# A down-projection by seven block products in place of eight, with token tiles in pairs

## The chip, the cores and the metric

The kernel runs on one core of one Trainium2 chip. The metric is the device time of one launch in microseconds (us). The kernel before takes 586.73 us (median of three runs, 585.8 to 587.77).

## What is computed

Two blocks follow each other, all in fp32: a gated linear recurrence (attention), and a Fourier mixing block with a two-layer projection behind it. Shapes: batch 4, 8 heads, 768 tokens, 48 channels a head, so 384 channels for the second block, and 1536 hidden units.

```python
f = 1 / (1 + exp(-f_logit))                        # attention, per batch and head
for t in range(S):
    state = f[t][:, None] * state + outer(k[t], v[t])
    y[t] = q[t] @ state
x = heads side by side                             # (4, 768, 384)
mixed = real(fft(fft(x, axis=1), axis=2))
u = x + mixed
un = (u - mean(u)) / sqrt(var(u) + 1e-6)           # over the channels
out = u + maximum(un @ w_ch1, 0) @ w_ch2           # 384 -> 1536 -> 384
```

The two weight matrices arrive as 64-bit floats and are turned into fp32 on the chip.

## The kernel before

**Units and batches.** Attention is done in 16 units, each a pair of heads of one batch; four units make a batch. Unit u's steps are, in order: exponentials on ScalarE (ACT), a scan on VectorE (DVE), more exponentials, the products `q` and `W` on DVE (L302, L303), 48 score matmuls `sc` (L314), a masked copy on DVE (L321), transposes `st` (L459), `ds` matmuls (L470), a state scan on DVE (L478), two sets of `y` matmuls (L490, L497), transposes `yt` (L517), and a fold of the tokens (DVE and GpSimd, POOL). The inputs of a unit are loaded by SP's queue: `f`, `k`, `q` two transfers each (L152), `v` one (L148).

**Fourier mixing and projection.** For each batch, `fnet` does four `z` steps (matmuls with a sequence table, L602), three `mix` steps (L618) whose results DVE adds to `x`, and the moments of each row. `turn` normalises a tile of 128 tokens into `un` (L653) and transposes it (`pt`, L656) into `unT`. A batch has six token tiles. Before, they go in two halves of three: for each half 12 steps `up`, each three matmuls with 384 moving columns (three tiles side by side, L690) and a ReLU on ACT into `h1` (L693), then for each of its three tiles 12 matmuls `po` (L700), a sum over the 12 blocks of hidden units with 384 output columns. DVE adds the sum to `x` (L704), and `store` writes the tile: tiles 1, 2, 3 and 5 by an indirect transfer from POOL's queue (L570), tiles 0 and 4 by SP (L576). Tile 4 comes last in its batch. Its rows go to two places, row 0 to one and rows 1 to 127 to the other.

**Buffers.** All PSUM tiles of `fnet` (`z`, `mix`, `pt`, `pp` of the up-projection, `po`) have the tag "f" and take turns in two buffers. `h1` has 13 buffers of 384 columns, the raw weights (`raw`) three.

**Weights and tables.** The weights come in 24 blocks of 384 KB. A word `C` converts one block (L209 and L210 on DVE, L219 and L220 on ACT, L222 on POOL); a word `c` looks at its smallest entry (L270 on DVE) and fetches a later block; `R` fetches the first three. The first 12 blocks are `w1`, the others `w2`. `tables` (word `T`) loads the tables of cosines: `seq_tab`'s first part with 128 rows (L157), its second with 127 rows (L158) and one row (L159), then the `wave` rows, 97, 63 and 33 of them (L170 to L172). `sort_tables` (word `S`) prepares them on POOL.

**What sets the order.** The text `ORDER` is a schedule written out by hand, and each engine executes its own instructions in the order in which they are issued there. A number is the next step of that unit, `F`b the next step of batch b's `fnet`, `H`b the next step of its `turns`, `L` a load (unit, then what), `G` clears a gap, `I` and `Z` set constants, `M` judges at the end whether the inputs ask for a second, slower way (the branch under `again`, which is not taken here).

Of the kernel before, what the change touches and what calls it, by code (L numbers as in the profile page):

```python
# [12 lines left out]
C = 128  # L13
# [30 lines left out]
)  # L44


@with_exitstack
def kernel(
# [36 lines left out]
    ph1 = ctx.enter_context(tc.tile_pool(name="ph1", bufs=13))  # L85
# [68 lines left out]
    def tables():  # L154


        nc.sync.dma_start(out=tab[:, 0, 0], in_=seq_tab[:, 0, 0])  # L157
        nc.sync.dma_start(out=tab[1:128, 0, 1], in_=seq_tab[1:128, 0, 1])  # L158
# [12 lines left out]
        nc.sync.dma_start(out=wave[1][0:63], in_=dim_tab[65:128, 1])  # L171
        nc.sync.dma_start(out=wave[1][63:QD], in_=dim_tab[0:QD - 63, 2])  # L172
        return wave
# [69 lines left out]
    def words(i):  # L243
        _, src, cols = blocks_of[i]
        raw = pr.tile([128, 384, 2], U32, tag="raw", name=f"raw{i}")
# [19 lines left out]
    def sizes():  # L265
# [7 lines left out]
        looked[0] += 1  # L273

# [53 lines left out]
    def attention_by_blocks(u, x_all):  # L328
# [8 lines left out]
        AD = ph1.tile([128, 2, NCH, 32], F32, tag="h1", name=f"ad{u}")  # L337
# [229 lines left out]
    def store(b, c, rows):  # L567
# [7 lines left out]
        for i, j, o in {0: [(0, C, 0)], 4: [(0, 1, 3 * QS), (1, C, HS + 1)]}[c]:  # L575
            nc.sync.dma_start(out=out[b, o:o + j - i], in_=rows[i:j])  # L576

    behind = {}

    def fnet(b, x, again=False):  # L580
# [66 lines left out]
        turned = [None, None]  # L647

        def turn(c):
            if c % 3 == 0:  # L650
                turned[c // 3] = p2.tile([128, 3, 3 * 128], F32, tag="unT", name=f"unT{b}_{c // 3}")
# [3 lines left out]
            for kt in range(3):  # L655
                nc.tensor.transpose(pt[:, kt * 128:(kt + 1) * 128], un[:, kt * 128:(kt + 1) * 128], ident)  # L656
            nc.scalar.copy(turned[c // 3][:, :, c % 3 * 128:(c % 3 + 1) * 128],  # L657
                           pt[:, :DM].rearrange("p (k t) -> p k t", k=3))

        def turns():  # L660
            for c in range(NCH):
                if c == 3:
                    for i in range(3, NCH):
                        moments(i)
                    deviation(slice(3, NCH))
                    yield
                turn(c)
                yield

        behind[b] = turns()  # L670
# [10 lines left out]
        for half in range(2):  # L681
            if again:
                for _ in behind[b]:
                    pass
            unT = turned[half]
            h1 = []
            for m in range(NF):
                pp = ps_f.tile([128, 512], F32, tag="f", name=f"up{b}_{half}_{m}")
                for kt in range(3):
                    nc.tensor.matmul(pp[:, :3 * 128], lhsT=w1[:, kt, m * 128:(m + 1) * 128], rhs=unT[:, kt],  # L690
                                     start=(kt == 0), stop=(kt == 2))
                h = ph1.tile([128, 3 * 128], F32, tag="h1", name=f"h1_{b}_{half}_{m}")
                nc.scalar.activation(h, pp[:, :3 * 128], AF.Relu)  # L693
                h1.append(h)
                yield
            for i in ((0, 1, 2), (0, 2, 1))[half]:
                c = 3 * half + i
                po = ps_f.tile([128, 512], F32, tag="f", name=f"po{b}_{c}")
                for m in range(NF):
                    nc.tensor.matmul(po[:, :DM], lhsT=h1[m][:, i * 128:(i + 1) * 128], rhs=w2[:, m],  # L700
                                     start=(m == 0), stop=(m == NF - 1))
                    if m in (3, 7):
                        yield
                nc.vector.tensor_tensor(x[:, c], po[:, :DM], x[:, c], ALU.add)  # L704
                store(b, c, x[:, c])
                yield

    x_of, units, fronts = {}, {}, {}
# [24 lines left out]
    with tc.manual_schedule():  # L733
        for word in ORDER.split():
# [5 lines left out]
            elif kind == "F":  # L740
                if n not in fronts:
                    fronts[n] = fnet(n, x_of.pop(n))
                next(fronts[n], None)
            elif kind == "H":
# [25 lines left out]
    with tc.If(again > 0):  # L770
        if wide:
            for i, (dst, _, _) in enumerate(blocks_of):
                single_or_zero(dst, words(i))
        nc.sync.dma_start(out=causal.rearrange("p (i n) -> p i n", n=32), in_=sel)
        for u in range(4):
            load(u, *("fkqv" if u < 3 else "qv"))
        for b in range(B):
# [4 lines left out]
            for _ in fnet(b, x, again=True):  # L782
                pass
# [69 lines left out]
```

## Time and profile before

| What | us |
|---|---|
| median of three runs | 586.73 |
| the profiled execution | 586.55 |
| its span, first to last instruction | 584.8 |
| PE (TensorE matmul) busy | 536.4 |
| DVE busy | 241.0 |
| ACT busy | 193.5 |
| POOL busy | 90.6 |

The span is what the profile sees, and the profiled execution's own time is 1.75 us longer. Busy times of the engines overlap, so they don't add up to the span. The trace leaves two records for each fp32 matmul: 288 matmuls of the up-projection stand as 576 rows of L690, and likewise for L700. A record's mean duration holds the pipeline's depth, so records that follow each other closely start at smaller distances than their mean durations. PEld is the loading of weights into PE, SPq the issuing of transfers by SP.

### The profile page before, as it was taken

To read this page: it belongs to the slowest core of one execution; us is meant where nothing else is said; L and a number is where in the kernel's file an instruction comes from. 1 tells how busy PE (TensorE), PEld (TensorE's weight loads), DVE (VectorE), ACT (ScalarE), POOL (GpSimd) and SP (SyncE) were. 2 spreads that over 40 slices of the span, in tenths; PEclk is the share of its full clock that TensorE was granted. 3 is DMA by queue.
4 is the path that set the end of the run, shared out by engine and by line. 5 is a ranking of instruction groups with operands and counts; after the bars stand their busy time and mean duration, and the time that the engine had idled before them with its cause. 6 is when DMAs were issued, how large, how long until landed. Compare 5 with 4: busy or idle time off the path is not lost.

```text
span 584.8 us, 8503 instructions
## 1 busy us (share of the span) xinstructions
PE 536.4 (92%) x3450; PEld 350.4 (60%) x3450; DVE 241.0 (41%) x431; ACT 193.5 (33%) x441; POOL 90.6 (15%) x147
## 2 busy tenths in 40 slices
PE   0778399999999999999999999999999999999991
PEld 0656276666566666766567666666565555555550
DVE  8997599975736334532526213111322020010000
ACT  5786057875425232631143301421123003102100
POOL 5335312434400000101100010220100000010010
PEclk9998599999999999999999999999999999999996
DMA  8974166651511021004300000000000000000000
GB/s 230 230 193 139 48 186 164 191 163 55 149 41 40 1 68 47 10 1 114 89 2 1 1 27 8 7 0 16 27 2 0 15 20 7 15 13 13 2 29 17
DMA packets 14785, 34.83 MB, mean 60 GB/s; under 512 B 2575, under 2 KB 4176, under 8 KB 14736
## 3 DMA queue, kind: packets, MB, share of 16 engines
q1 hardware_dynamic: 13632, 30.65, 19.5%
q0 software_dynamic: 1104, 3.54, 1.7%
q8 instruction: 29, 0.48, 0.4%
q14 instruction: 20, 0.16, 0.1%
HBM read 29.46 MB, written 4.72 MB: 58 GB/s over the span
## 4 chain that ended last, share of the span: by engine, by line
PE 84%; DMA 3%; DVE 3%; ACT 3%; SPq 2%; issue 2%; POOL 1%; ACTq 0%; DVEq 0%; POOLq 0%
PE up L690 33%; PE po L700 32%; PE z L602 4%; PE sc L314 3%; PE y L490 3%; PE y L497 2%; PE mix L618 2%; DMA q<-in_qkf_dram 2%; PE pt L656 1%; PE ds L470 1%; PE yt L517 1%; SPq L171 1%; DMA v<-in_v_dram 1%; PE st L459 1%; DMA g<-in_qkf_dram 1%
## 5 line engine op out<-in xcount | busy, mean ns | idle before, releaser
L690 PE MATMUL up<-unT,w 128*128 128x384 f32 x576 | 195.1, 490 | 1.3 <-ACT h L693 0.6
L700 PE MATMUL po<-w,h 128*128 128x384 f32 x576 | 189.8, 487 | 0.0
L700 PEld LDWEIGHTS po<-w,h 128*128 128x128 f32 x576 | 108.2, 190 | 73.4 <-issue 0.3
L690 PEld LDWEIGHTS up<-unT,w 128*128 128x128 f32 x576 | 106.8, 190 | 71.7 <-issue 1.2
L693 ACT ACTIVATE h<-up 128x384 f32<-128x384 f32 x96 | 46.9, 489 | 197.7 <-PE up L690 197.5
L704 DVE TENSOR_TENSOR x<-po,x 128x384 f32<-128x384 f32 x24 | 13.4, 557 | 156.5 <-PE po L700 156.5
L314 PE MATMUL sc<-q,W 48*64 48x128 f32 x768 | 29.1, 302 | 27.7 <-DVE W L303 23.1
L570 POOL DMA_INDIRECT out_dram<-x,place x16 | 16.5, 1033 | 229.2 <-DVE x L704 216.4
L314 PEld LDWEIGHTS sc<-q,W 48*64 48x64 f32 x768 | 24.3, 149 | 33.0 <-issue 15.7
L321 DVE COPY_PREDICATED at<-causal,sc 128x768 f32<-128x768 uint32 x32 | 31.4, 1034 | 16.9 <-PE sc L314 16.9
L222 POOL TENSOR_TENSOR w<-w,raw 128x384 uint32<-128x384 uint32 x24 | 27.5, 1148 | 52.2 <-ACT raw L220 41.0
L290 DVE TENSOR_TENSOR_SCAN W<-g,bound 112x768 f32<-112x768 f32 x16 | 28.2, 1761 | 8.6 <-PE st L459 7.6
L490 PE MATMUL y<-at,v 128*64 128x128 f32 (+1 forms) x384 | 27.0, 294 | 0.0
L490 PEld LDWEIGHTS y<-at,v 128*64 128x64 f32 (+1 forms) x384 | 23.2, 140 | 4.2 <-issue 3.4
L302 DVE TENSOR_TENSOR q<-q,g 112x768 f32<-112x768 f32 x16 | 16.7, 1041 | 20.3 <-ACT g L295 12.8
L292 POOL COPY deep<-W 112x1 f32<-112x1 f32 x16 | 5.4, 338 | 123.4 <-DVE W L290 123.2
L478 DVE TENSOR_TENSOR_SCAN stt<-ds,te 112x288 f32<-112x288 f32 x16 | 11.9, 751 | 28.6 <-PE ds L470 28.6
L497 PE MATMUL y<-q,stt 48*48 48x128 f32 x320 | 21.3, 276 | 0.0
L497 PEld LDWEIGHTS y<-q,stt 48*48 48x48 f32 x320 | 17.9, 159 | 5.0 <-issue 3.3
L657 ACT COPY unT<-pt 128x384 f32<-128x384 f32 x24 | 11.4, 481 | 25.2 <-PE pt L656 25.2
L618 PE MATMUL mix<-cd,zz 96*128 96x192 f32 (+5 forms) x128 | 18.4, 331 | 0.7 <-ACT h L693 0.5
L210 DVE SCALAR_TENSOR_TENSOR w<-raw,w 128x384 uint32<-128x384 uint32 x24 | 17.8, 742 | 0.8
(116 smaller groups left out, 486.6 us busy)
## 6 DMA issues: line engine op xcount, KB each, us to landing
raw<-in_w_ch_dram SPq DMA_DIRECT2D x24, 384.0 KB
v<-in_v_dram SPq DMA_DIRECT2D x16, 288.0 KB
g<-in_qkf_dram SPq DMA_DIRECT2D x32, 144.0 KB
q<-in_qkf_dram SPq DMA_DIRECT2D x32, 144.0 KB
k<-in_qkf_dram SPq DMA_DIRECT2D x32, 144.0 KB
out_dram<-x SPq DMA_DIRECT2D x4, 192.0 KB
out_dram<-x SPq DMA_DIRECT2D x4, 190.5 KB
out_dram<-x,place POOLq DMA_INDIRECT x16, 2.6
```

The source lines that it names most:

```text
L210: nc.vector.scalar_tensor_tensor(bits, hi, 0xC0000000, bits, ALU.bitwise_and, ALU.bitwise_or)
L222: nc.gpsimd.tensor_tensor(bits, bits, lo, ALU.add)
L290: nc.vector.tensor_tensor_scan(W, g, bound[:R], 0.0, ALU.add, ALU.min)
L314: nc.tensor.matmul(ps[64 * s:64 * s + 64, r, i * C:(i + 1) * C], lhsT=W[ROWS[r], o + 64 * s:o + 64 * s + 64], rhs=Q[ROWS[r], o:o + C], sta ...
L321: nc.vector.copy_predicated(AT[:, :, half], causal.bitcast(U32).unsqueeze(1).unsqueeze(1).to_broadcast([128, 2, NCH // 2, C]), ps[:, :, :N ...
L490: nc.tensor.matmul(y[FILL[r], c * C:(c + 1) * C], lhsT=vt[:, c, r * D:r * D + (64 if r == 0 else D)], rhs=AT[:, r, c], start=(c % 4 == 0), ...
L497: nc.tensor.matmul(y[ROWS[r], c * C:(c + 1) * C], lhsT=st[ROWS[r], :, c - 1], rhs=Q[ROWS[r], c * C:(c + 1) * C], start=False, stop=True, s ...
L602: nc.tensor.matmul(z[:, cols], lhsT=src[:, j, lo:hi], rhs=tab[:, t, T % 2, cols], start=(i == 0), stop=(i == len(parts) - 1), skip_group_c ...
L618: nc.tensor.matmul(mix[rows, o], lhsT=zz[:rows_of[T], T, j:j + rows.stop - rows.start], rhs=cd[:rows_of[T], T, :NQ - odd], start=(i == 0), ...
L690: nc.tensor.matmul(pp[:, :3 * 128], lhsT=w1[:, kt, m * 128:(m + 1) * 128], rhs=unT[:, kt], start=(kt == 0), stop=(kt == 2))
L693: nc.scalar.activation(h, pp[:, :3 * 128], AF.Relu)
L700: nc.tensor.matmul(po[:, :DM], lhsT=h1[m][:, i * 128:(i + 1) * 128], rhs=w2[:, m], start=(m == 0), stop=(m == NF - 1))
```

## The change

**Seven products.** The token tiles go in pairs, (0, 3), (2, 5) and (1, 4), and the hidden units in two halves of six blocks. For a pair, the ReLU outputs are four blocks h11, h21 (first half of the hidden units, first and second tile) and h12, h22 (second half), and `w2` is four blocks w11, w12 (first half of the hidden units, left and right 192 output columns) and w21, w22. The plain way takes eight block products. The new function `combine` (word `W`, once) makes, on DVE,

T1 = w12 - w11, T2 = w22 - T1, T3 = w22 - w12, T4 = w21 - T2,

and `projected` makes for each pair, on DVE as well,

S1 = h21 + h22, S2 = S1 - h11, S3 = h11 - h21, S4 = h12 - S2.

With seven products, in the order in which they are issued, P1 = h11 w11, P2 = h12 w21, P4 = h22 T4, P5 = S1 T1, P6 = S2 T2, P3 = S4 w22, P7 = S3 T3, the results are

first tile, left: P1 + P2; right: P1 + P6 + P5 + P3; second tile, left: P1 + P6 + P7 + P4; right: P1 + P6 + P7 + P5.

Each product is six matmuls of 192 moving columns. The sums are kept in two PSUM tiles, `fx` (P1, to which P6 and then P7 are added, and P2) and `fz` (P4, and P5 with P3). DVE adds each part to `x` as it becomes ready, and the last addition (`both`) adds the sum of P1, P6 and P7 to both halves of the second tile.

**What goes with it.** `up` steps have 256 moving columns (two tiles) and `h1` two buffers of six blocks. The first pair of the first batch still takes the plain way, 24 matmuls of 384 columns, since its turn comes before all of `w2` is there. `fnet` ends after the `mix` steps, and the rest of a batch has the word `P`: 20 steps a pair, 12 `up` and then eight. `turns` and the moments are regrouped for the pairs. The order is new from its first word on: `R` comes first, and `W` after the second pair's last `up` step. Tile 4 still comes last in its batch.

**Row sixteen.** The 127 rows of tile 4's second store, and the 127 rows of one load of `seq_tab`, are cut into rows 1 to 15 and 16 to 127.

```diff
 ORDER = (
-    "Gq0 L0v Gq2 Gk2 Gq3 I L0f 0 Gk1 Gk0 L1f L0q Gq1 0 L1k i 1 L0k R Z 0 L1q 1 0 1 C C L3fk c 0 0 0 L2f "
...
+    "R Gk0 I Gq0 i L0f Gq1 L1f Gq2 Gk2 Z L2q Gq3 L0q C L2f C Gk1 L0k C c c 0 0 1 0 1 0 C L1k L1q L2v 0 "
+    "L0v c 0 1 0 L2k 2 C L3fk 0 1 L1v c 0 1 0 3 C 0 2 1 1 L3v 3 2 1 1 3 2 0 L3q 1 3 2 2 L4fk 4 c 3 3 "
+    "L5fk 2 1 0 3 C C 2 2 T 2 1 2 L4qv 3 4 c c 1 3 5 L6fk 3 c 2 4 L5qv 3 3 5 4 2 5 4 4 4 3 5 6 S 4 C 4 4 "
...
+    "P2 P2 P2 P2 F3 P2 P2 F3 F3 P2 F3 P2 P2 P2 F3 P2 P2 P2 P2 P2 P2 P2 P2 P2 H3 P2 P2 P2 H3 P2 P2 P2 H3 "
+    "P2 P2 P2 P2 P2 F3 F3 P2 P2 P2 P2 H3 P2 P2 P2 P2 P3 P3 P3 H3 H3 P3 P3 P3 P3 P3 P3 P3 P3 P3 P3 P3 P3 "
+    "P3 P3 P3 P3 P3 P3 P3 P3 P3 P3 P3 H3 P3 P3 P3 P3 P3 P3 H3 P3 P3 P3 P3 P3 P3 P3 P3 P3 P3 P3 P3 P3 P3 "
+    "P3 P3 M P3 P3 P3 P3 P3 P3 P3 P3 P3 P3 P3 P3"
 )
+
+PAIRS = ((0, 3), (2, 5), (1, 4))
...
-    ph1 = ctx.enter_context(tc.tile_pool(name="ph1", bufs=13))
+    ph1 = ctx.enter_context(tc.tile_pool(name="ph1", bufs=2))
...
-        nc.sync.dma_start(out=tab[1:128, 0, 1], in_=seq_tab[1:128, 0, 1])
+        nc.sync.dma_start(out=tab[1:16, 0, 1], in_=seq_tab[1:16, 0, 1])
+        nc.sync.dma_start(out=tab[16:128, 0, 1], in_=seq_tab[16:128, 0, 1])
...
+    def combine():
+        H = NF // 2
+        w11, w12, w21, w22 = [w2[:, i * H:(i + 1) * H, j * HD:(j + 1) * HD] for i in range(2) for j in range(2)]
+        t2, t3, t4 = [pr.tile([128, H, HD], F32, tag="raw", name=f"block{i}") for i in range(3)]
+        tt = nc.vector.tensor_tensor
+        tt(t3, w22, w12, ALU.subtract)
+        tt(w12, w12, w11, ALU.subtract)
+        tt(t2, w22, w12, ALU.subtract)
+        tt(t4, w21, t2, ALU.subtract)
+        blocks[1], blocks[2], blocks[4] = w11, w21, t4
+        blocks[5], blocks[6], blocks[3], blocks[7] = w12, t2, w22, t3
...
-        for i, j, o in {0: [(0, C, 0)], 4: [(0, 1, 3 * QS), (1, C, HS + 1)]}[c]:
+        for i, j, o in {0: [(0, C, 0)], 4: [(0, 1, 3 * QS), (1, 16, HS + 1), (16, C, HS + 16)]}[c]:
...
+    def projected(b, x, again=False):
+        H = NF // 2
+        tt = nc.vector.tensor_tensor
+        for j, (c, d) in enumerate(PAIRS):
...
+            unT = turned_of[b][j].rearrange("p k t n -> p k (t n)")
+            hs = []
             for m in range(NF):
-                pp = ps_f.tile([128, 512], F32, tag="f", name=f"up{b}_{half}_{m}")
+                if m % H == 0:
+                    hs.append(ph1.tile([128, H, 2, 128], F32, tag="h1", name=f"h1_{b}_{j}_{m}"))
+                pp = ps_f.tile([128, 512], F32, tag="f", name=f"up{b}_{j}_{m}")
                 for kt in range(3):
-                    nc.tensor.matmul(pp[:, :3 * 128], lhsT=w1[:, kt, m * 128:(m + 1) * 128], rhs=unT[:, kt],
+                    nc.tensor.matmul(pp[:, :256], lhsT=w1[:, kt, m * 128:(m + 1) * 128], rhs=unT[:, kt],
                                      start=(kt == 0), stop=(kt == 2))
...
+                nc.scalar.activation(hs[-1][:, m % H].rearrange("p t n -> p (t n)"), pp[:, :256], AF.Relu)
                 yield
...
+            h11, h21, h12, h22 = [hs[k][:, :, t] for k in range(2) for t in range(2)]
+            c1, c2, d1, d2 = [x[:, i, o:o + HD] for i in (c, d) for o in (0, HD)]
+
+            def product(i, out, h, start=False):
+                for m in range(H):
+                    nc.tensor.matmul(out, lhsT=h[:, m], rhs=blocks[i][:, m], start=(start and m == 0),
+                                     stop=(m == H - 1), skip_group_check=True)
+
+            fx = ps_f.tile([128, 512], F32, tag="f", name=f"fx{b}_{j}")
+            X, Y = fx[:, :HD], fx[:, HD:2 * HD]
+            product(1, X, h11, start=True)
+            s1 = p1.tile([128, H, 128], F32, tag="s1", name=f"s1_{b}_{j}")
+            tt(s1, h21, h22, ALU.add)
+            tt(h21, h11, h21, ALU.subtract)
+            yield
+            product(2, Y, h12)
+            tt(c1, X, c1, ALU.add)
+            tt(h11, s1, h11, ALU.subtract)
+            yield
+            fz = ps_f.tile([128, 512], F32, tag="f", name=f"fz{b}_{j}")
+            V, Z = fz[:, :HD], fz[:, HD:2 * HD]
+            product(4, V, h22, start=True)
+            tt(c1, Y, c1, ALU.add)
+            tt(h12, h12, h11, ALU.subtract)
+            yield
+            product(5, Z, s1)
+            tt(d1, V, d1, ALU.add)
+            yield
+            product(6, X, h11)
+            tt(d2, Z, d2, ALU.add)
+            yield
+            product(3, Z, h12)
+            tt(c2, X, c2, ALU.add)
+            yield
+            product(7, X, h21)
+            tt(c2, Z, c2, ALU.add)
+            store(b, c, x[:, c])
+            yield
+            both = x[:, d].rearrange("p (a n) -> p a n", a=2)
+            tt(both, X.unsqueeze(1).to_broadcast([128, 2, HD]), both, ALU.add)
+            store(b, d, x[:, d])
+            yield
```

More of the change, by code (lines that the diff above doesn't have):

```diff
@@ L656, in turn @@
                 nc.tensor.transpose(pt[:, kt * 128:(kt + 1) * 128], un[:, kt * 128:(kt + 1) * 128], ident)
-            nc.scalar.copy(turned[c // 3][:, :, c % 3 * 128:(c % 3 + 1) * 128],
-                           pt[:, :DM].rearrange("p (k t) -> p k t", k=3))
+            nc.scalar.copy(turned[j][:, :, t], pt[:, :DM].rearrange("p (k t) -> p k t", k=3))
         def turns():
[L661 to L665, printed above, removed]
-                    yield
-                turn(c)
+            for j, (c, d) in enumerate(PAIRS):
+                if j == 0:
+                    turn(c)
+                    yield
+                    moments(d)
+                    deviation(slice(d, d + 1))
+                elif j == 1:
+                    moments(4)
+                    moments(5)
+                    deviation(slice(4, 6))
+                    yield
+                    turn(c)
+                else:
+                    turn(c)
                 yield
-        behind[b] = turns()
+                turn(d)
+                yield
+        behind[b], turned_of[b] = turns(), turned
         for c in range(3):
@@ L679, in fnet @@
             yield
-        for half in range(2):
+    def projected(b, x, again=False):
+        H = NF // 2
+        tt = nc.vector.tensor_tensor
+        for j, (c, d) in enumerate(PAIRS):
             if again:
[L683 to L686, printed above, removed]
+                for _ in range((3, 3, 2)[j]):
+                    next(behind[b], None)
+            unT = turned_of[b][j].rearrange("p k t n -> p k (t n)")
+            hs = []
@@ L708 @@
-    x_of, units, fronts = {}, {}, {}
+            if not again and (b, j) == (0, 0):
+                for t, i in enumerate((c, d)):
+                    po = ps_f.tile([128, 512], F32, tag="f", name=f"po{b}_{i}")
+                    for m in range(NF):
+                        nc.tensor.matmul(po[:, :DM], lhsT=hs[m // H][:, m % H, t], rhs=w2[:, m],
+                                         start=(m == 0), stop=(m == NF - 1))
+                        if m in (2, 5, 8):
+                            yield
+                    tt(x[:, i], po[:, :DM], x[:, i], ALU.add)
+                    store(b, i, x[:, i])
+                    yield
+                continue
@@ L773 @@
                 single_or_zero(dst, words(i))
+        else:
+            for i, (dst, src, cols) in enumerate(blocks_of):
+                nc.sync.dma_start(out=dst, in_=src[:, cols])
+        combine()
         nc.sync.dma_start(out=causal.rearrange("p (i n) -> p i n", n=32), in_=sel)
@@ L781 @@
                     pass
-            for _ in fnet(b, x, again=True):
+            for _ in fnet(b, x):
+                pass
+            for _ in projected(b, x, again=True):
                 pass
```

42 lines of the change are left out of this document (20 added, 22 removed), and 26 rows, old and new, of the table ORDER.

## The prediction

> **What bounds the kernel now.** I read the page's slices first, then the busy times of stretches, then the chain that ended last, the waits, and single instructions.
>
> ```profile
> span 584.8 us, 8503 instructions
> ...
> PE   0778399999999999999999999999999999999991
> ...
> DVE  8997599975736334532526213111322020010000
> ...
> DMA  8974166651511021004300000000000000000000
> ```
>
> Forty slices of 14.6 us. VectorE (DVE) is full in the first third, TensorE (PE) from the sixth slice on, and the last slice is nearly empty. So there are three stages. I cut them at the first down-projection matmul (125.6) and at the last (572.2):
>
> ```profile
> 0.00:67.00 67.00, 35.06 (x545) 29.23 (x546) 52.62 (x73) 41.06 (x81) 30.03 (x66) 0.93 0.70 183
> 67.00:125.60 58.60, 57.08 (x518) 40.99 (x519) 55.67 (x103) 38.68 (x88) 17.55 (x17) 0.94 0.57 155
> 125.60:572.20 446.60, 444.25 (x2388) 280.13 (x2387) 132.15 (x256) 113.76 (x272) 43.00 (x65) 1.00 0.10 30
> 572.20:584.80 12.60, 0.00 (x0) 0.00 (x0) 0.56 (x1) 0.00 (x0) 0.00 (x0) 0.65 0.05 18
> ```
>
> (Columns: stretch, length, busy PE, PEld, DVE, ACT, POOL, granted clock, share of the 16 DMA engines, GB/s.) **Stage A**, to 125.6: DVE works 52.62 + 55.67 = 108.3 and idles 17.3. PE is busy in its second half too, but what PE still lacks there is made by DVE. **Stage B**: PE is busy 444.25 of 446.6 at full clock; every record taken away counts. **Stage C**: one addition, then 12 us of almost nothing.
>
> That DVE has no lead at 125.6 is seen in the size checks of the weights (a `c` word each): up to 92.15 and from there to 125.6 they are
>
> ```profile
> L270 DVE TENSOR_REDUCE small<-raw 128x1 f32<-128x384 f32 x8 | 4.3, 543 | 0.0
> ```
>
> ```profile
> L270 DVE TENSOR_REDUCE small<-raw 128x1 f32<-128x384 f32 x12 | 6.3, 542 | 0.0
> ```
>
> 20 together, just the number of `c` words ahead of the first projection step in the order. DVE and PE reach that point together.
>
> **Stage A, part by part.** The largest single idle time of DVE:
>
> ```profile
> DVE q L302 <- DMA q<-in_qkf_dram: 7.5, 1, 7.5
> ```
>
> ```profile
> 42.40 0.29 SPq L158 DMA_DIRECT2D tab<-in_seq_tab_dram  x1
> ...
> 47.22 6.27 SPq L171 DMA_DIRECT2D wave<-in_dim_tab_dram  x1
> ...
> 54.85 0.91 SPq L152 DMA_DIRECT2D q<-in_qkf_dram  x2
> ```
>
> ```profile
> 55.36 9.44 DMA q<-in_qkf_dram
> ```
>
> ```profile
> 47.00:50.00 3.00, 2.63 (x46) 2.15 (x45) 2.06 (x6) 1.67 (x6) 1.21 (x4) 1.00 0.07 24
> ```
>
> L158 loads 127 rows, and behind it SP's issues stall (6.27 for one). Meanwhile the DMA share is 0.07, about one engine of 16, at 24 GB/s. L158's 191.5 KB at that rate are 8.0 us, the 97 rows of `wave` (145.5 KB) 6.1, and the q rows queued behind them land at 55.36 + 9.44 = 64.8. The diff cuts L158 at row 16 into 15 and 112 rows. If those spread, 8 us leave that engine, and the 7.5 us wait goes with them. Two issues instead of one cost SP 0.3 us, with slack. The next late thing is then `wave`, still 97 rows, and the new order puts L4qv behind the tables in place of L5qv; between the tables and its use (`4`, u4's product) stand two scans, a state scan, three size checks and a fold on DVE, over 7 us, about what `wave` takes. So the wait goes to 0, or to 7.5 if this cover fails. I take 0.
>
> DVE work ahead of the first projection, counted from both orders: one `C`, one `c`, one state scan and two normalisations fewer, all else the same.
>
> ```profile
> L210 DVE SCALAR_TENSOR_TENSOR w<-raw,w 128x384 uint32<-128x384 uint32 x24 | 17.8, 742 | 0.8
> ...
> L270 DVE TENSOR_REDUCE small<-raw 128x1 f32<-128x384 f32 x24 | 12.8, 544 | 0.0
> L478 DVE TENSOR_TENSOR_SCAN stt<-ds,te 112x288 f32<-112x288 f32 x16 | 11.9, 751 | 28.6 <-PE ds L470 28.6
> L653 DVE TENSOR_SCALAR un<-x,mv,rstd 128x384 f32<-128x384 f32 x24 | 10.9, 472 | 13.2 <-PE pt L656 8.4 <-ACT rstd L645 4.8
> L209 DVE TENSOR_SCALAR w<-raw 128x384 uint32<-128x384 uint32 x24 | 10.0, 417 | 4.0 <-DMA raw<-in_w_ch_dram 3.9
> ```
>
> 0.417 + 0.742 + 0.544 + 0.751 + 2 x 0.472 = 3.4. The `R` word moves ahead of everything: three weight blocks land before the first gate rows, which come later, but DVE then has `C` work in its place; I cost it at 0 (between -2 and +3). The first projection starts at 125.6 - 7.5 - 3.4 = **114.7**.
>
> **Stage B, part by part.** The chain has long runs of PE records (each fp32 matmul leaves two):
>
> ```profile
> 112.52 0.58 PE yt L517 x6
> ...
> 117.36 0.48 PE st L459 x5
> 117.84 0.78 PE ds L470 x16
> ...
> 128.17 1.26 PE y L497 x20
> ...
> 185.61 1.31 PE mix L618 x8
> ...
> 476.31 9.69 PE up L690 x30
> ...
> 548.95 23.23 PE po L700 x72
> ...
> 572.21 0.56 DVE x L704
> ```
>
> A 384-column record takes 23.23/72 = 0.3226, a 192- or 193-column one 1.31/8 = 0.164: per column nearly the same, 0.840 and 0.852 ns. So a 256-column record is 0.2165 (0.215 to 0.218 by either rate).
> - Down-projection. Before, 24 tiles x 24 records x 0.3226 = 185.8. After, two tiles stay (15.5), and 11 pairs take 7 products x 12 records x 0.164 = 13.78 each, 151.5. Sum 167.0: **-18.8**.
> - Up-projection left in stage B: before 7 halves x 72 x 0.3226 = 162.6; after 11 pairs x 72 x 0.2165 = 171.5: **+8.9**. (The other 7.6 of the narrower first pair lie in stage A, where DVE decides: worth nothing.)
> - By the orders, an `st`, a `ds`, a `yt` and two transposes now come after the cut, a `y` before it: 0.48 + 0.78 + 0.58 + about 0.8 - 1.26 = **+1.4**.
> - A new wait. `fx` and `fz` take turns in two PSUM buffers with everything else named "f". The tile after a pair therefore takes `fx`, and must wait for the last addition (`both`), which itself waits for the seventh product. Behind the waiting matmul stands all of PE. Where attention words follow the pair they cover it; by the order four pair ends have none (b2's second and third, b3's first and second).
>
> ```profile
> L700 PE MATMUL po<-w,h 128*128 128x384 f32 x576 | 189.8, 487 | 0.0
> ...
> L704 DVE TENSOR_TENSOR x<-po,x 128x384 f32<-128x384 f32 x24 | 13.4, 557 | 156.5 <-PE po L700 156.5
> ...
> L302 DVE TENSOR_TENSOR q<-q,g 112x768 f32<-112x768 f32 x16 | 16.7, 1041 | 20.3 <-ACT g L295 12.8
> ```
>
> ```profile
> L545 DVE TENSOR_TENSOR eo<-eo 128x192 f32<-128x192 f32 x16 | 5.7, 358 | 5.3 <-POOL eo L543 4.4
> ```
>
>   One addition 0.557, the pipeline's lost overlap 0.487 - 0.323 = 0.16, signals 0.1 (the chain shows 0.03 between 572.18 and L704's start, and there is one each way): 0.8 x 4 = **+3.3**.
> - DVE gets, per pair, four sums of 768 (1.04), six half additions (0.36) and `both` (0.56): 6.9 for 1.1 before. Hidden behind 13.8 of products; 11 pairs and `W` (four operations of 1152 elements, an estimate of 1.5 each from the 768 row) add about 70 to 132.15 of 446.6. Where attention work is queued ahead of the sums, products wait: I put **+1** on this and on ReLU, whose cover per step shrinks from 1.94 to 1.30; up to 8 if the cover is gone. The ReLU outputs now have two buffers in place of 13; a pair's first ReLU waits for the seventh product before it, which PE has finished 1.30 (one up step) earlier: 0.
>
> Sum: 446.6 - 18.8 + 8.9 + 1.4 + 3.3 + 1 = 442.4; PE ends at 114.7 + 442.4 = 557.1.
>
> **Stage C.** The last store is 127 rows too (L576).
>
> ```profile
> 576.00:580.00 4.00, 0.00 (x0) 0.00 (x0) 0.00 (x0) 0.00 (x0) 0.00 (x0) 0.50 0.08 29
> ...
> 582.00:583.00 1.00, 0.00 (x0) 0.00 (x0) 0.00 (x0) 0.00 (x0) 0.00 (x0) 0.50 0.03 11
> ```
>
> ```profile
> 510.00 0.36 SPq L576 DMA_DIRECT2D out_dram<-x  x1
> ```
>
> ```profile
> 511.00:511.50 0.50, 0.50 (x3) 0.25 (x2) 0.00 (x0) 0.00 (x0) 0.00 (x0) 1.00 0.80 298
> 511.50:512.00 0.50, 0.50 (x3) 0.32 (x2) 0.00 (x0) 0.00 (x0) 0.00 (x0) 1.00 0.00 0
> ```
>
> Share 0.08 again, until about 582.5, and 2.3 more to the end. A store of 128 rows issued at 510.0 had moved all by 511.5. No trace shows 15 or 112 rows: the ends are 12.05 (no gain) and 3.5; I take the 128-row store: two issues ahead 0.5, 1.5, then 2.3, sum 4.4 after the addition. The Trainium skill ("DMA: Bandwidth & Descriptors", the section on why a DMA increments its semaphore by 16) says that a transfer runs on the largest number of engines up to 16 that divides its rows, 127 giving one; by it 15 rows would take 15 engines and 112 all 16. The trace agrees for 127 rows, with shares of 0.07 and 0.08, and shows neither of the others.
>
> End: 557.1 + 0.6 + 4.4 = 562.1 of span. The profiled execution took 586.55 for its span of 584.8, 1.75 around it, and stands 0.2 under the median 586.73. Forecast **564**.
>
> **Rivals.**
> 1. *The forecast*, 558 to 570: 0.60.
> 2. *Stage A gains little*: q still comes late behind `wave`, or raw weights do; 7.5 to 10 stay: about 573. For it: slices 1 to 3 have DMA at 9, 9 and 8 too. Chance 0.16.
> 3. *Stage A gains more*: 17.3 of idle time leave 9.8 after my cut; weight blocks first may fill part of them: about 556. Chance 0.12.
> 4. *The row-sixteen cuts don't spread*, so the change does not do what it says: 7.5 and 7.6 stay: 579. Chance 0.05.
> 5. *Sums late* (W and attention ahead of them on DVE): 571. Chance 0.04.
> 6. *Slower: the weight load becomes the bound of the narrow products.* The rows give one load
>
> ```profile
> L618 PEld LDWEIGHTS mix<-cd,zz 96*128 96x128 f32 x32 | 5.4, 189 | 0.0
> L700 PEld LDWEIGHTS po<-w,h 128*128 128x128 f32 x576 | 108.2, 190 | 73.4 <-issue 0.3
> ```
>
>   as 0.19. It hides under a record of 0.3226, but from 0.19 downward it would decide: 924 product records x 0.026 = 24, and 564 + 24 = 588. Against it: the `mix` records have such loads and still run at 0.164. For it: their weights have 96 rows, not 128. Chance 0.02.
> 7. *Loads don't overlap at all.* The change adds 684 records (1836 for 1152), each with its load; bare, 0.19 each, that is 130 more: 694. But 72 records of `po` in 23.23 leave no room for 72 bare loads of 0.19. Chance 0.01. The Trainium skill ("TensorE: Matmul & The Clock Gate", Part 3, The mechanism) says that a weight load overlaps matmuls in flight only when the row group differs, which here it doesn't; by that rule this rival would hold, and the `po` run contradicts it.
>
> **How the numbers follow.** The prediction is rival 1's 564. The range takes it with 2, 3 and 5: 554 to 575, leaving out about 0.15. Faster by over 0.3%, about what a measurement of this kernel can tell from no change, is under 585: rivals 1 to 5, 0.97, less 0.01 for several misses together: 0.96. Slower: 6 and 7, 0.03. Same: 0.01.
>
> **What would show it.** Stage A: first `po` near 115, DVE's wait for q gone, SP's issues of `wave` short. Stage B: runs of 12 product records at 1.97, up steps of 6 at 1.30, PE idle of about 0.65 before L690 at four pair ends, released by DVE. Stage C: about 4.4 between the last addition and the end. The forecast falls if products run at 0.19 a record, if DVE stays the bound past the first pair, or if the end still shows one engine's share.

## The result, and the profile after

The changed kernel takes 569.27 us (median of four runs, 568.03 to 570.39). The kernel before took 587.01 on the same chip. The ratio is 0.9699, with a 95% interval of 0.9672 to 0.9726: about 17.7 us faster. The forecast was 564, with a range of 554 to 575.

The page of the changed kernel: its span, the busy times, and the forty slices, now of 14.2 us.

```profile
span 567.9 us, 10060 instructions
...
PE 522.7 (92%) x4134; PEld 455.6 (80%) x4134; DVE 301.0 (53%) x534; ACT 204.2 (36%) x497; POOL 87.4 (15%) x147
...
PE   0577689999999999999999999999999999999993
...
DVE  8997798885896564543837074224442250303130
...
DMA  7938436566002101404100000000000000000001
```

PE works 13.7 us less than before, although it now has 4134 records. DVE works 60 us more, and its digits show these sums after the tenth slice. The cut into stages, at the first down-projection matmul (119.0) and at the last (558.6), by the busy times of stretches:

```profile
0.00:67.00 67.00, 36.79 (x545) 30.53 (x545) 56.98 (x79) 41.18 (x81) 29.46 (x66) 0.91 0.71 198
67.00:119.00 52.00, 49.31 (x501) 39.70 (x501) 47.39 (x91) 36.10 (x89) 12.31 (x16) 0.92 0.50 139
119.00:558.60 439.60, 436.56 (x3090) 385.34 (x3088) 196.12 (x366) 126.94 (x328) 45.61 (x66) 1.00 0.11 32
558.60:567.90 9.30, 0.00 (x0) 0.00 (x0) 0.55 (x1) 0.00 (x0) 0.00 (x0) 0.76 0.16 48
```

| Stage | before | forecast | after | forecast missed by |
|---|---|---|---|---|
| A, to the first down-projection matmul | 125.6 | 114.7 | 119.0 | +4.3 |
| B, to the last | 446.6 | 442.4 | 439.6 | -2.8 |
| C, behind the last addition | 12.05 | 4.4 | 8.75 | +4.35 |

The misses add up to 5.85, which is, but for rounding, the distance between the measured span, 567.9, and the forecast one, 562.1. (The 125.6 is where the chain puts that matmul. Its record starts at 125.4, and 119.0 is such a start, so A and B each carry 0.2 of this difference.) Three steps were wrong, not one: two misses of about equal size went one way, and the one in stage B went the other way and hid part of them. The experiments ask what each part of the change was worth.

### The profile page after: what moved, and what is told of

The parts are those of the page before. It is cut to its first block, busy times and chain, and to the rows that moved or that the text cites. A ratio compares the mean times of both kernels' runs of the same rounds, so it can differ in the third digit from the quotient of the medians.

```text
span 567.9 us, 10060 instructions
## 1 busy us (share of the span) xinstructions
PE 522.7 (92%) x4134; PEld 455.6 (80%) x4134; DVE 301.0 (53%) x534; ACT 204.2 (36%) x497; POOL 87.4 (15%) x147
## 4 chain that ended last, share of the span: by engine, by line
PE 77%; DVE 10%; DMA 6%; issue 2%; ACT 1%; SPq 1%; POOL 1%; ACTq 0%; DVEq 0%; POOLq 0%
PE up L730 32%; PE fx L753 15%; PE fz L753 11%; PE sc L337 3%; PE z L625 3%; PE y L513 3%; PE mix L641 3%; DMA v<-in_v_dram 2%; PE y L520 2%; PE ds L493 2%; PE po L739 2%; DMA raw<-in_w_ch_dram 1%; DVE W L313 1%; DVE at L344 1%; PE pt L680 1%
## 5 line engine op out<-in xcount | busy, mean ns | idle before, releaser
L730 PE MATMUL up<-unT,w 128*128 128x256 f32 x864 | 199.7, 384 | 0.6 <-ACT h L732 0.2
L730 PEld LDWEIGHTS up<-unT,w 128*128 128x128 f32 x864 | 160.9, 191 | 25.4 <-issue 1.7
L732 ACT ACTIVATE h<-up 128x256 f32<-128x256 f32 x144 | 54.8, 382 | 173.2 <-PE up L730 158.3
L337 PE MATMUL sc<-q,W 48*64 48x128 f32 x768 | 29.2, 301 | 22.2 <-DVE W L326 18.7
L753 PE MATMUL fx<-block,h 128*128 128x192 f32 x264 | 46.8, 327 | 0.0
L337 PEld LDWEIGHTS sc<-q,W 48*64 48x64 f32 x768 | 24.4, 149 | 26.6 <-DVE W L326 18.7
L753 PE MATMUL fx<-w,h 128*128 128x192 f32 x264 | 45.1, 327 | 0.7 <-DVE x L708 0.5
L753 PEld LDWEIGHTS fx<-w,h 128*128 128x128 f32 x264 | 43.1, 190 | 1.7 <-PE mix L641 0.9
L753 PEld LDWEIGHTS fx<-block,h 128*128 128x128 f32 x264 | 43.3, 190 | 0.5 <-DVE q L325 0.2
L753 PE MATMUL fz<-w,h 128*128 128x192 f32 x132 | 23.5, 328 | 0.1
L520 PEld LDWEIGHTS y<-q,stt 48*48 48x48 f32 x320 | 18.7, 161 | 6.0 <-DVE stt L501 2.8
L753 PE MATMUL fz<-block,h 128*128 128x192 f32 x132 | 23.4, 327 | 0.0
L753 PE MATMUL fz<-w,s 128*128 128x192 f32 x132 | 23.2, 326 | 0.0
```

The source lines that it names most:

```text
L337: nc.tensor.matmul(ps[64 * s:64 * s + 64, r, i * C:(i + 1) * C], lhsT=W[ROWS[r], o + 64 * s:o + 64 * s + 64], rhs=Q[ROWS[r], o:o + C], sta ...
L520: nc.tensor.matmul(y[ROWS[r], c * C:(c + 1) * C], lhsT=st[ROWS[r], :, c - 1], rhs=Q[ROWS[r], c * C:(c + 1) * C], start=False, stop=True, s ...
L730: nc.tensor.matmul(pp[:, :256], lhsT=w1[:, kt, m * 128:(m + 1) * 128], rhs=unT[:, kt], start=(kt == 0), stop=(kt == 2))
L732: nc.scalar.activation(hs[-1][:, m % H].rearrange("p t n -> p (t n)"), pp[:, :256], AF.Relu)
L753: nc.tensor.matmul(out, lhsT=h[:, m], rhs=blocks[i][:, m], start=(start and m == 0), stop=(m == H - 1), skip_group_check=True)
```

## Experiments

Each kernel below ran beside the kernel before on its own chip. Differences "to the changed kernel" are the difference of the two ratios times 587.0 us; 0.0027 on either side of a ratio is 1.6 us. Unless said otherwise, the edits are made to the changed kernel.

### The products alone: eight_products

```diff
-            if not again and (b, j) == (0, 0):
+            if not again:
...
             elif kind == "W":
-                combine()
+                pass
```

> Every pair takes the plain way of the first one (eight block products, one 384-column matmul per tile and row block); the four operations that combine the weight blocks are left out; order, pairs and cuts stay. Theory P (the seven products are the gain of the middle stage): 11 pairs x (15.48 - 13.78) = +18.7 us, 588 us, level with the kernel before, because pairs cost 8.9 us in narrower up-projection. Rival Q (the sums on DVE and their waits give part of it back): +12 us or less, 581 us or less. Rival R (the gain lies in the new order and the cuts alone): within 2 us of 569.3.

Measured: 588.64 us, ratio 1.0017 (1.0003 to 1.0030), so 18.7 us more than the changed kernel. Theory P holds: with pairs and everything else, but eight products, the kernel is no faster than before. That 18.7 is the expected number to the tenth is partly chance. In the traces stage B is 20.9 longer with eight products (460.5 for 439.6), and PE is busy 20.0 longer in it (456.6 for 436.6). The end takes 2.0 of that back. The last addition and SP's issues with eight products:

```profile
580.42 0.56 DVE L743 TENSOR_TENSOR x<-po,x 128x384 f32<-128x384 f32 x1 [7.18 <-PE po L739]
581.01 1.04 SPq L599 DMA_DIRECT2D out_dram<-x  x3
```

SP issues at once there, and the end behind the addition is 6.7 (587.7 - 580.98), against 8.75. The extra 60 us of sums on DVE take nothing back in stage B: PE idles 3.0 there, and 3.9 with eight products. The timeline of the changed kernel shows that the seven run at full speed:

```profile
428.80 1.98 PEld L753 LDWEIGHTS fz<-w,h 128*128 128x128 f32 x12
428.96 2.11 PE L753 MATMUL fz<-w,h 128*128 128x192 f32 x12
...
430.75 1.98 PEld L753 LDWEIGHTS fx<-block,h 128*128 128x128 f32 x12
430.91 2.11 PE L753 MATMUL fx<-block,h 128*128 128x192 f32 x12
```

Twelve records start within 1.95 (430.91 - 428.96), 0.1625 each. Their twelve weight loads are shown at 190 ns each, yet all twelve stand in 1.98.

### The cut of the store: store_uncut

```diff
-4: [(0, 1, 3 * QS), (1, 16, HS + 1), (16, C, HS + 16)]}[c]:
+4: [(0, 1, 3 * QS), (1, C, HS + 1)]}[c]:
```

> The last store's 127 rows go out as one transfer again. By the price of the prediction the cut is worth 12.05 - 4.4 = 7.6 us: 577 us. Theory S (after the cut the end is no longer set by the store but by SP's own load of the flag and its branch, which the long transfer used to hide): the end goes from 8.75 to 12.05 + 0.9 (the wait for tile 1's indirect store stays), +4.2 us, 573.5 us. Rival (the row count doesn't matter): 569.3 us, one issue less.

Measured: 588.56 us, ratio 1.0016 (0.9999 to 1.0034), 18.6 us more. None of the three expectations named anything like it: this one cut is worth as much as the seven products. The end is 12.9 long (586.9 - 573.99), 4.2 more than with the cut, as theory S said. The other 14.8 are lost in stage B. First the waits of all engines from 119 to 560 (engine, what it does, whom it waits for: total, times, longest), then the chain of waits around the first of them (start, length, what):

```profile
ACT x L542 <- DMA out_dram<-x: 13.3, 2, 9.1
```

```profile
221.02 2.56 DMA out_dram<-x,place
...
224.02 9.87 DMA out_dram<-x
...
233.99 0.65 ACT x L542
...
234.68 0.73 PE st L482 x5
```

The tiles `x` of the batches have two buffers, so batch 2's first unit is copied (ACT, L542) into the buffer that batch 0's last store still reads. That store takes 9.87 us as 127 rows. ACT waits for it, twice, 13.3 in all (the second time batch 3's copy for batch 1's store). PE's own waits from 200 to 573 follow:

```profile
PE pt L680 <- ACT h L732: 7.8, 1, 7.8
PE st L482 <- ACT x L542: 3.1, 1, 3.1
```

ReLUs and copies stand behind the waiting copy on ACT, and PE stands behind them: 10.9. PE's idle time in the stage grows by as much, from 3.0 to 13.9. The remaining 3.9 are the granted clock, the third column from the right here:

```profile
230.00:235.00 5.00, 1.92 (x27) 1.36 (x26) 2.75 (x4) 0.93 (x2) 0.19 (x1) 1.00 0.52 136
235.00:240.00 5.00, 5.00 (x19) 4.13 (x18) 0.00 (x0) 1.70 (x6) 0.00 (x0) 0.66 0.41 120
...
360.00:370.00 10.00, 2.18 (x11) 1.62 (x10) 0.00 (x0) 1.20 (x3) 0.63 (x1) 0.75 0.05 19
370.00:380.00 10.00, 10.00 (x95) 7.89 (x95) 3.50 (x6) 1.28 (x4) 1.45 (x4) 0.74 0.01 2
```

After each gap PE runs at about 0.7 for some microseconds: 0.66 over 5 us and 0.74 over 10 lose 1.7 and 2.6, which is about the 3.9 by which PE's busy time in stage B is longer (440.5 here, 436.56 with the cut). Together 10.9 + 3.9 + 4.2 = 19.0, the difference of the two spans (586.9 and 567.9). The old order left room here. The waits of ACT in the kernel before:

```profile
ACT x L519 <- DMA out_dram<-x: 4.1, 2, 2.7
```

There PE waited for none of these copies: no wait of PE behind 115 is put down to them or is longer than 0.6 in all.

### The cut of the load, and the next one: table_uncut, wave_cut

```diff
-        nc.sync.dma_start(out=tab[1:16, 0, 1], in_=seq_tab[1:16, 0, 1])
-        nc.sync.dma_start(out=tab[16:128, 0, 1], in_=seq_tab[16:128, 0, 1])
+        nc.sync.dma_start(out=tab[1:128, 0, 1], in_=seq_tab[1:128, 0, 1])
```

> The 127 rows of the sine table are loaded by one transfer again. By the prediction's term q for u4 lands about 8 us later and DVE's wait, now 2.0, grows to about 9: +7.5 us, 577 us. Rival A (stage A is bound by the other waits of DVE, which the late q would swallow): +2 us or less, 571 us or less. In between, 572 to 575: the wait returns, and part of what followed it was waiting anyway.

Measured: 575.32 us, ratio 0.9797 (0.9768 to 0.9825), 5.8 more. The first down-projection matmul starts at 124.2, 5.2 later. DVE's waits up to 118 in this run, then in the changed kernel:

```profile
DVE q L324 <- DMA q<-in_qkf_dram: 6.4, 1, 6.4
DVE x L704 <- PE mix L640: 3.4, 3, 1.6
```

```profile
DVE x L705 <- PE mix L641: 3.0, 3, 1.6
DVE eo L568 <- POOL eo L566: 2.6, 1, 2.6
DVE q L325 <- DMA q<-in_qkf_dram: 2.0, 1, 2.0
```

So the cut spreads the load and the wait for q comes back without it. 2.0 of that wait are left, behind the `wave` rows.

```diff
-        nc.sync.dma_start(out=wave[0][0:QD + 1], in_=dim_tab[0:QD + 1, 0])
+        nc.sync.dma_start(out=wave[0][0:QD], in_=dim_tab[0:QD, 0])
+        nc.sync.dma_start(out=wave[0][QD:QD + 1], in_=dim_tab[QD:QD + 1, 0])
```

> The 97 rows of the channel table are loaded as 96 and 1. Theory W (the 2.0 us that DVE still waits for q are these rows, on one DMA engine): q lands about 5 us earlier, the first projection starts 2 us earlier, 567.3 us. Rival B (another wait takes its place, or PE and the raw weights set the pace): within 0.7 us of 569.3.

Measured: 569.35 us, ratio 0.9689 (0.9662 to 0.9717): rival B. The wait for q is gone, but the first down-projection matmul starts only 0.7 earlier, at 118.3, and the run as a whole is not faster. The 2.0 of DVE's wait taken away here are not 2.0 gained.

### Who sets stage A: fewer_checks, short_up

```diff
         if wide:
-            nc.vector.tensor_reduce(small[:, i:i + 1], raws[i][:, :, 1].bitcast(F32), mybir.AxisListType.X,
-                                    ALU.min, apply_absolute_value=True)
+            if i >= 19:
+                nc.vector.tensor_reduce(small[:, i:i + 1], raws[i][:, :, 1].bitcast(F32), mybir.AxisListType.X,
+                                        ALU.min, apply_absolute_value=True)
             fetch()
```

> The size checks of the first 19 weight blocks, all ahead of the first down-projection, are left out (their loads are still fetched at the same places): 19 x 0.543 = 10.3 us less work on DVE in the first stage, nothing less on PE. Theory D (the prediction's premise: DVE sets the first stage to its end): 7 to 10 us less, 559 to 562 us. Rival E (from 95 us on, where PE is busy 23.93 of 24 us, PE sets it, and DVE only before): 3 us or less, 566 us or more.

```diff
-                for kt in range(3):
+                last = 0 if not again and (b, j) == (0, 0) else 2
+                for kt in range(last + 1):
                     nc.tensor.matmul(pp[:, :256], lhsT=w1[:, kt, m * 128:(m + 1) * 128], rhs=unT[:, kt],
-                                     start=(kt == 0), stop=(kt == 2))
+                                     start=(kt == 0), stop=(kt == last))
```

> The first pair's up-projection takes one of its three row blocks (two thirds of that product are left out): 12 x 4 records x 0.2165 = 10.4 us less work on PE ahead of the first down-projection, nothing less on DVE. Theory D (DVE sets the first stage): 0 to 2 us less, 567 us or more. Rival E (PE sets its last 24 us): 5 to 10 us less, 559 to 564 us.

The first kernel leaves out 19 size checks, the second two of the three row blocks of the first pair's up-projection. Measured: 10.3 us less of DVE give 567.98 us, ratio 0.9676 (0.9658 to 0.9694), which this run can't tell from the changed kernel; the first down-projection matmul is 2.2 earlier (116.8). 10.4 us less of PE give 565.50, ratio 0.9628 (0.9612 to 0.9644), 4.2 less, and that matmul is 4.2 earlier (114.8). One trace places this matmul only roughly: in `store_uncut`, `no_second_way`, `short_tail` and `eight_products`, whose edits come later than stage A, it starts between 118.3 and 119.9. So the 4.2 is clear of this scatter, the 2.2 barely. Theory D falls, and E holds only in part: neither engine alone sets the stage. The last 23 us of it, first in the changed kernel, then with less PE work:

```profile
95.00:118.00 23.00, 22.93 (x247) 18.35 (x246) 20.57 (x38) 17.00 (x44) 6.57 (x7) 1.00 0.51 152
```

```profile
95.00:118.00 23.00, 18.31 (x204) 12.49 (x197) 22.27 (x41) 18.61 (x44) 7.82 (x8) 0.93 0.61 176
```

PE is full in the first and DVE nearly so. Take PE's work away, and DVE is full at once. (The second stretch holds the first 3.2 us of down-projection too, since that starts at 114.8.)

### The head of the order: weights_later, gates_first

```diff
-    "R Gk0 I Gq0 i L0f Gq1 L1f Gq2 Gk2 Z L2q Gq3 L0q C L2f ..."
+    "Gk0 I Gq0 i L0f Gq1 L1f Gq2 Gk2 Z L2q Gq3 L0q R C L2f ..."
```

> The word that fetches the first three weight blocks moves from the head of the order to just before the first conversion, as the kernel before had it later too. The prediction's term is 0, between -2 and +3: within 2 us of 569.3. If the weights at the head are worth the DVE work they allow while the first gates load, this is slower by up to 5 us; if the 5.4 us by which PE's first scores come later (18.7 for 13.3) are a loss, it is faster by up to 5 us.

Measured: 574.69 us, ratio 0.9783 (0.9764 to 0.9802), 4.9 more; the first down-projection matmul starts at 124.0, 5.0 later. DVE's first waits in this run:

```profile
DVE w L214 <- DMA raw<-in_w_ch_dram: 6.3, 4, 4.3
```

```diff
-    "R Gk0 I Gq0 i L0f Gq1 ..."
+    "I L0f R Gk0 Gq0 i Gq1 ..."
```

> The first gate rows are loaded ahead of the first three weight blocks, which stay ahead of everything else. Theory G (both matter: the gates start ACT's and PE's chain, the weights fill DVE meanwhile): PE's first scores come about 4 us earlier than 18.7, 1 to 3 us less, 566 to 568 us. Rival H (what counts is that the weights are there before DVE has other work): 0 to 2 us more, 569 to 571 us.

Measured: 569.02 us, ratio 0.9691 (0.9673 to 0.9708): the same as the changed kernel. The first down-projection matmul starts at 117.8, 1.2 earlier, little more than the scatter. G's step did not happen: PE's first scores start at 18.7 in both. In the order DVE has three conversions and two size checks ahead of unit 0's work, so earlier gates may meet a busy DVE; this is argued, not shown. In `fewer_checks`, without those two checks, the scores start at 18.2. The conversions were not taken away.

### The two cuts in the kernel before: before_cuts

> The kernel before with nothing changed but the two cuts at row sixteen. By the prediction's prices 7.5 for the wait for q and 7.6 for the end: 15.1 us less than before, 572 us. By what the cuts were worth singly in the changed kernel (5.9 for the table; 3.3 to 4.2 at the end, and nothing in the middle, where PE of the kernel before waits for no store): 9 to 10 us less, 577 us. Rival (stage A of the kernel before is bound by PE too): 5 us or less, 582 us.

Measured: 575.05 us, ratio 0.9786 (0.9761 to 0.9811), 12.6 us less than before. That lies between the two sums. The profiles give 10.7 (584.8 and 574.1): 5.3 in stage A (first down-projection matmul at 120.1 for 125.4), 5.1 behind the last addition (574.1 - 567.14 = 6.96 for 12.05), nothing of note in stage B. So the cuts bring most of the gain of the change, 12.6 of 17.7, when put into the old kernel alone. All the rest of the change brings 5.1 on top of them: with the cuts in both, the pairs and the new order with eight products (`eight_products`) are 13.6 slower than the old layout, and the seven products win 18.7. In the new kernel the cuts bring more, because it needs the buffer sooner: ACT waits 13.3 for the uncut store there, and 4.1 in the old one.

### The end: no_second_way, short_tail, small_edits

In the first of these everything from the load of the flag to the end of the branch is deleted.

> The load of the flag, the branch and the whole second way behind it are left out; the first way and its stores stay. Theory S (SP's load of the flag and its branch set the end after the cut of the store): the end goes from 8.75 to about 6.3 after the last addition, 2 to 3 us less, 566.5 to 567.3 us. Rival T (the store's landing sets the end): within 0.7 us of 569.3.

Measured: 564.87 us, ratio 0.9625 (0.9609 to 0.9641), 4.3 less. The end behind the last addition is 4.4 (563.0 - 558.60). Theory S holds, with a larger price than it named. The end by the timelines, first of the changed kernel, then of this one (tile 1's store, the last addition, SP's three issues):

```profile
557.27 0.96 POOL L593 DMA_INDIRECT out_dram<-x,place  x1 [25.65 <-DVE x L783]
558.59 0.56 DVE L787 TENSOR_TENSOR x<-fx,x 128x384 f32<-128x384 f32 x1 [1.59 <-PE fx L753]
560.08 2.07 SPq L599 DMA_DIRECT2D out_dram<-x  x3
```

```profile
556.73 0.96 POOL L593 DMA_INDIRECT out_dram<-x,place  x1 [25.64 <-DVE x L783]
558.04 0.56 DVE L787 TENSOR_TENSOR x<-fx,x 128x384 f32<-128x384 f32 x1 [1.59 <-PE fx L753]
559.33 1.04 SPq L599 DMA_DIRECT2D out_dram<-x  x3
```

SP starts 0.9 and 0.7 behind the addition, once tile 1's store has landed, and needs 2.07 or 1.04 for the three issues. Most of the difference, 3.1 of 4.35, comes after them. The instructions of the branch on SP in the changed kernel (count, duration in ns, first and last start), then those of the barrier at the end:

```profile
L857 SPq EVENT_SEMAPHORE  x8: 17/17/17, 565.7 to 566.2; - x8
...
L857 SPq COMPARE_BRANCH  x1: 50/50/50, 563.1 to 563.1; - x1
```

```profile
L941 SPq EVENT_SEMAPHORE  x14: 17/28/28, 566.3 to 567.9; - x14
```

The branch is taken at 563.1, and SP's next instruction starts at 565.7: 2.6 for the jump over the second way. That SP waits for nothing else in this time is not shown by these rows alone, but ACT takes the same branch 17.6 us earlier and has the same gap (545.5 to 548.1), and POOL nearly so (557.6 to 560.3). From the last issue's end to the end of the span it is 5.75 (567.9 - 562.15) with the branch and 2.63 (563.0 - 560.37) without. In the kernel before the same jump lay under the transfer; SP's branch, then its semaphores behind it:

```profile
L770 SPq EVENT_SEMAPHORE  x8: 17/17/17, 577.0 to 583.1; - x8
...
L770 SPq COMPARE_BRANCH  x1: 50/50/50, 574.4 to 574.4; - x1
```

There too 2.6 pass, from 574.4 to 577.0, but then SP waits for the store until 583.1.

```diff
-            nc.sync.dma_start(out=out[b, o:o + j - i], in_=rows[i:j])
+            queue = nc.scalar if b == B - 1 and j <= 16 else nc.sync
+            queue.dma_start(out=out[b, o:o + j - i], in_=rows[i:j])
...
+            elif kind == "V":
+                again = nc.values_load(flag[0:1, 0:1], min_val=0, max_val=1)
     tc.no_sync_barrier()
-    again = nc.values_load(flag[0:1, 0:1], min_val=0, max_val=1)
```

With these two edits, the 112 rows first, and the products in the order 1, 2, 5, 6, 3, 4, 7:

> Three edits at the end of the changed kernel. The products run in the order 1, 2, 5, 6, 3, 4, 7, so that the pair's first tile is stored one product earlier and SP's last store no longer waits for it; in the last batch the two small stores go out by ACT's queue, the 112 rows by SP's, first; the flag is loaded a few products ahead of the end. Theory S (SP's wait of 0.9, two issues of 1.5 together and its load of 0.9 stand ahead of its branch): 1.5 to 3.3 us less, 566.0 to 567.8 us. Rival T (every engine's branch, DVE's first, sets the end at the same time): within 0.7 us of 569.3.

Measured: 567.59 us, ratio 0.9673 (0.9638 to 0.9707); the interval is too wide to tell it from the changed kernel. The end behind the last addition is 6.3 (566.1 - 559.82), against 8.75, but one of the three edits did nothing:

```profile
557.31 0.36 DVE L781 TENSOR_TENSOR x<-fz,x 128x192 f32<-128x192 f32 x1 [3.54 <-PE fz L754]
...
557.95 0.96 POOL L593 DMA_INDIRECT out_dram<-x,place  x1 [25.64 <-DVE x L785]
...
560.55 0.33 SPq L600 DMA_DIRECT2D out_dram<-x  x1
560.57 0.90 ACTq L600 DMA_DIRECT2D out_dram<-x  x2
```

The first tile's last part is in P3's half of `fz`, but its addition waits until P4, which writes the other half, is done (557.31, where P4's records end). Tile 1's store starts no earlier than before, and SP's still waits for it, 0.73 behind the last addition. So the last kernel drops the new order of the products, keeps the other two edits, and takes the order of `gates_first`:

> The changed kernel with the first gate rows ahead of the first weight blocks, the flag loaded a few products ahead of the end, and the last batch's two small stores on ACT's queue behind SP's 112 rows; the products in their old order, since the new order of the run before saved nothing (SP's store still started 0.73 after the last addition). If these add up: 1.7 for the end and 0.3 for the start, 567.3 us, and the end after the last addition is 6.3. Rival: the end is worth nothing by itself and the gain of that run was chance: 569 us.

Measured: 566.42 us, ratio 0.9643 (0.9626 to 0.9660). Its interval lies below that of the changed kernel: 3.3 us less, faster than both kernels. The end is 6.5 (566.2 - 559.74), 2.25 shorter. The first down-projection matmul starts at 119.8, so this trace shows no gain from the head of the order. The trace is of the longest of the five runs, and its span is only 1.7 shorter than the changed kernel's; where the rest of the 3.3 comes from is not shown.

## Why the prediction was right, and where it was not

**The products: right.** The step says 18.8, and eight_products measures 18.7 as a whole. Records of 192 columns take 0.1625 where the step took 0.164; with that, 924 records make the step 20.2, and stage B shows it (20.0 of PE's busy time). The seven products lose some of it again at the end, which the prediction did not connect with them. Six records of an up step stand in 1.31 on the chain, as forecast. Rivals 6 and 7 fall with the rows at 428.80. The Trainium skill ("TensorE: Matmul & The Clock Gate", Part 3, The mechanism) says that a weight load overlaps matmuls in flight only when the row group differs; these rows contradict that, as the old `po` run did. The same section lets a load into the background weight buffer go ahead as well, and whether these loads use it no run here shows.

**The new wait: wrong, 3.3 too much.** The failing step is "The tile after a pair therefore takes `fx`". The chain of the changed kernel at one of the four pair ends that the step named, b2's second (no wait of PE in the whole stage is put down to a last addition):

```profile
429.12 1.95 PE fz L753 x12
431.07 1.95 PE fx L753 x12
433.02 1.31 PE up L730 x6
```

The up step follows at once, and in the timeline DVE's additions lie like this:

```profile
431.11 0.36 DVE L783 TENSOR_TENSOR x<-fz,x 128x192 f32<-128x192 f32 x1 [1.59 <-PE fz L753]
...
433.06 0.56 DVE L787 TENSOR_TENSOR x<-fx,x 128x384 f32<-128x384 f32 x1 [1.59 <-PE fx L753]
```

The up step runs while the last addition still reads `fx`, so it must have the buffer of `fz`, whose last reader is done at 431.47 (the trace names no buffers). The two buffers went by which came free first, not by turns, so the words "take turns" in the description of the buffers are wrong as well. Without this term the sum is 439.1; measured is 439.6. That is close in its parts too: PE's busy time fell by 7.7 where the sum has 8.5, and its idle time grew by 0.7 where the sum, without the new wait, has 1.

**Stage A: right in sign, wrong in premise.** "DVE and PE reach that point together" was read off the size checks, and then only DVE's microseconds were counted. The 7.5 for q were worth 5.3 in the old kernel and 5.2 in the new one. DVE work taken away is worth about a fifth of itself (2.2 of 10.3 by the trace, less by the whole time), so the 3.4 counted in full should have been about 0.7, an estimate. The head of the order, put at 0 with bounds of -2 and +3, is worth 5.0, outside those bounds. And PE's 7.6 in the narrower first pair, "worth nothing", lies where 10.4 of PE's work are worth 4.2. These singles add up to more than the 6.4 that stage A gained (record starts 125.4 and 119.0): from before_cuts (120.1) to the changed kernel (119.0) only 1.1 is left for all of the new order and the narrower pair together, weights first included. Something else in the new order gives some microseconds back. Which move it is no run here separates; that stays open.

**The end: wrong, 4.35 too little.** The sum was 0.5 for issues, 1.5 for the transfer and 2.3 to the end (4.3 in all, written as 4.4). The 2.3 was read from a trace in which SP's branch had long been taken when the transfer landed. With the short transfer the branch comes last. Without the branch the end measures 4.4, the forecast number, but by luck: it is made of 0.7 until SP starts, 1.04 for the issues and 2.63 behind them, where the forecast had 0, 0.5 and 3.8. The changed kernel adds to this 3.1 behind the last issue, 1.0 in the issues (the third took 1.4) and 0.2 ahead of them. The 0.7 to 0.9 ahead of the issues are the wait for tile 1's store, which in the new pairs comes one product before tile 4's.

**Rival 4: its price was wrong, and its side.** "The row-sixteen cuts don't spread" was priced at 7.5 and 7.6, 579 us. Undone singly, the cuts cost 5.8 and 18.6. Had neither spread, and if the two add up, which no run here shows, the time would be near 594, slower than before. The prediction looked for the store's 9 us only at the end, not at who needs the buffer that it reads.

**The number.** 569.27 is near the upper end of the 558 to 570 of rival 1. The misses of stage A and of the end, 8.65 together, were offset by 2.8 in stage B; that part of the closeness is luck. Even without it the time would have stayed below the 575 of the range.

## What to carry to other kernels

A slow transfer out of a rotating buffer is paid where the buffer is next written, not only at the end: when an order is made tighter, look at the waits that were just short of reaching the bound engine (here 4.1 us on ACT, none on PE). Where two engines are both nearly full, the idle time or the work of one is worth only a part of itself, and a test that takes ten microseconds from each tells which part. When the last wait of a program is cut, ask what ran under it: here a taken branch.

## What was not expected of the hardware

- A taken branch over the second way's code cost SP 2.6 us in both kernels, and ACT as much, though the compare itself takes 50 ns. The Trainium skill ("Runtime: NRT & Kernel Launch", Instruction fetch mechanics) says that a branch whose target is outside the window of fetched instructions waits for a fetch; the gap agrees with it, and no run here shows the fetch itself.
- A gap of 3.1 us on PE was followed by a granted clock of 0.66 over the next 5 us, and one of 7.8 by 0.74 over the next 10. In store_uncut this added 3.9 to 10.9 of waiting.
- DVE's addition from one half of a PSUM tile waited for a product into the other half: with P3 done, it started at 557.31, where P4 ended (short_tail). Whether the chip needs this wait, or only the program's semaphores ask for it, no run here shows.
